# Attention with a memory, then a three-way max layer: weights assembled in PSUM, queries loaded twice, softmax sums by unit, another instruction order

## The chip, the cores and the metric

The kernel runs on one core of one Trainium2 chip. The core has a matrix engine (TensorE, PE in the profile; PEld is its loading of stationary operands), a vector engine (VectorE, DVE), a scalar engine (ScalarE, ACT), a general engine (GpSimd, POOL) and a queue for transfers (SyncE, SP). Each engine works through its own list of instructions in order, and engines wait for one another by semaphores. SBUF is the working memory with 128 partitions. PSUM holds eight banks of 512 float32 values per partition; matmuls write there. The metric is the device time of one execution in microseconds, less is better.

## The reference

Four batches, eight heads, 576 positions, 64 values per head. Causal attention is mixed with a read from a memory by a gate per head, and the result goes through a layer that takes the largest of three products:

```python
scores = q @ k^T / sqrt(D), causal          # B, H, S, D = 4, 8, 576, 64
a = exp(scores - max); a /= a.sum(-1) + 1e-9
local = a @ v
q_p = where(q > 0, q, exp(q) - 1) + 1       # phi(q)
mem_out = (q_p @ M_prev) / (q_p . z_prev + 1e-6)
g = sigmoid(beta)                            # one per head
x = (g * mem_out + (1 - g) * local)          # [2304, 512]
h = max(x @ w1, x @ w2, x @ w3)              # each [512, 768]
out = h @ w_out                              # [768, 512]
```

## The kernel before

**Tiling.** A batch is cut into two halves of the sequence: positions 0 to 319 (a "top" block of 64 rows and two units of 128) and 320 to 575 (two units of 128). A pair is one batch, one half and two heads, so there are 32 pairs and 64 steps of one head each. Pairs 0 to 7 are batch 0. The program (loop at line 890) goes through the steps. In step n it computes the scores of head n, transposes the probabilities of head n-1, multiplies by the values for the pair that ended in step n-2, and prepares the next pair. Once the four pairs of a half are done, the half's layer ("MoE" in the code) is queued: 18 upward products (6 column blocks times w1, w2, w3) of 12 matmuls each, and two or three downward products. They are handed out by a quota over the next eight steps (`run_moe`, line 873), so matmuls of the layer fill the time between those of attention.

**Split numbers.** For accuracy, most operands of matmuls are split into a high part (fp32r, a rounded float32) and a low part, the rest. A product is then three matmuls: high x high, low x high, high x low.

**Weights (`load_weights`, line 503).** The weights come in 24 chunks of 128 x 512 (18 of w1, w2, w3, 6 of w_out), read as 64-bit words in two 32-bit halves. For each chunk ScalarE scales the upper half into a tile `g` in SBUF. VectorE shifts `g` left by 3, ors in the lower half's upper bits (line 517), and ors in the sign (line 521). So a float32 is put together from the halves. Then ScalarE or VectorE makes the high part, and GpSimd or VectorE subtracts for the low part. One chunk each is prepared in steps 4 to 8 (`EARLY_STEPS`), and from then on two before each upward product (`PER_PIECE`), so the program lists all of them before the eleventh product. The raw chunks go through a ring of three buffers `r_w`, in which later also the raw keys and queries of pairs 8 to 31 lie.

**Queries and keys.** For pairs 0 to 3 the product of queries and keys is one float32 matmul. From pair 4 on a query tile `qs` holds 64 features twice over 128 partitions, since the keys' high and low parts lie in the two halves of the partitions. In pairs 4 to 7 the queries are transposed on PE, from pair 8 (`FLIP`) on VectorE in 32 x 32 blocks, after eight loads that place keys and queries. Both heads of a pair lie in the two halves of one transposed tile. So `split_in` (line 629) makes high and low part on the 64 partitions where a head lies, and then copies both across to the other 64 (line 642).

**Softmax.** `scores` masks and finds the maximum on VectorE, ScalarE takes the exponential with its sum. After the second unit of a head, VectorE adds 1e-9 to both units' sums and takes both reciprocals (`inverse`, line 678), and GpSimd multiplies both units by them and by the gate (`normal`, line 684). `phi` (line 529) works out phi(q) and its product with z: a reduction on VectorE, then an add of 1e-6 and a reciprocal.

**PSUM.** Eight banks: two for scores (`bs`), two for transposes (`bt`), one for the value product (`bv`), three for the layer (`bm`).

**Order of the instructions.** Nothing is issued as it is written. A planner (`Plan`) notes each operation with its operands, and `emit` (line 243) then goes through a simulated time: each operation has a cost (line 147) and delays after its inputs (`AFTER`, line 78), and each engine takes, among what is ready, what stands first in the program. Where an operation may run on one of two engines, the planner picks the one that would finish first, VectorE with a penalty of 1000 ns (`PEN`). Early on, where PE would idle over 400 ns, small "filler" matmuls are put in (line 280). They end when the bank that they write, the third of `bm`, is used for the first time. Nearly all operations are issued by line 297, so groups in the profile are told apart by the tiles: `g` and `rw` are weights, `wh`, `wl`, `woh`, `wol` their high and low parts, `p` probabilities, `pt` their transposes, `sum` softmax sums, `nn` phi's norms, `rk` transposed keys and queries, `k` the split keys, `t` the layer's maximum.

Of the kernel before, what the change touches and what calls it, by code (L numbers as in the profile page):

```python
# [67 lines left out]
class Plan:  # L68
# [18 lines left out]
    PEN = {"dve": 1000}  # L87

# [111 lines left out]

    def note(self, can):
# [41 lines left out]
    def emit(self):  # L243
# [6 lines left out]
        last = 0.0  # L250

        def place(op):
# [13 lines left out]
        for _ in self.ops:  # L266
# [56 lines left out]
def attention_memory_moe(ctx, tc, q, k, v, m_prev, z_prev, beta, w1, w2, w3, w_out, out):  # L323
# [14 lines left out]
    EARLY_STEPS, PER_PIECE = range(4, 9), 2  # L338
# [23 lines left out]
    r_e = Ring(cp, 2, [128, 384], F32, "phe")  # L362
    r_f = Ring(cp, 2, [128, 384], F32, "phf")

    r_k = Ring(cp, 2, [128, 512], F32, "rk")
    r_q0 = Ring(cp, 2, [128, 3, 2, D], F32, "rq")
# [11 lines left out]
    r_sum = Ring(cp, 6, [128, 2, 2], F32, "sum")  # L378
# [6 lines left out]
    b_m = Ring(ps, 3, [128, 512], F32, "bm")  # L385
# [13 lines left out]
    def load_qk(pi):  # L399
# [12 lines left out]
        else:  # L412
            t = f(r_w.next())
            r["k"], r["qt"] = t[:, : hf.n], t[:, 512 : 512 + hf.n]
            for src, to in ((k, r["k"]), (q, r["qt"])):
                for i in range(4):
# [3 lines left out]
                            b, 2 * hp + i // 2, hf.t0 : hf.t0 + hf.n, 32 * (i % 2) : 32 * (i % 2) + 32  # L420
                        ].rearrange("(c p) d -> p c d", p=32),
                    )
        t = r_q0.next()[:, : len(hf.blocks)]
        if hf.top:
            P.sp.dma_start(out=t[:, 0], in_=q[b, hs, 0:128, :].rearrange("h p d -> p h d"))
        for e in range(2):
            t0 = hf.t0 + hf.units[0][1]
            P.sp.dma_start(
                out=t[:, hf.top :, e],
                in_=q[b, 2 * hp + e, t0 : t0 + 256, :].rearrange("(c p) d -> p c d", p=128),  # L430
            )
        r["q"] = t
# [36 lines left out]
    nc.gpsimd.tensor_copy(out=qs_all[:, :64], in_=mask[:, :64])  # L469
    for e in range(2):  # L470
# [32 lines left out]
    def load_weights(n):  # L503
        for _ in range(min(n, len(wchunks))):
            src, dh, dl = wchunks.popleft()
# [6 lines left out]
            bits = g.bitcast(U32)  # L512
            P.act.activation(out=g, in_=f(words[:, :, 1]), func=AF.Copy, scale=2.0**-111)
# [8 lines left out]
                out=bits, in0=words[:, :, 1], scalar=0x80000000, in1=bits,  # L522
                op0=ALU.bitwise_and, op1=ALU.bitwise_or,
            )
            P.copy(("act", "dve"), out=dh, in_=gv)
            P.combine(("pool", "dve"), ALU.subtract, out=dl, in0=gv, in1=f(dh))


    def phi(pi):
# [7 lines left out]
        ev, fv = (  # L537
# [168 lines left out]
    def scores(pi, e, u):  # L706
# [21 lines left out]
        if i == 0:  # L728
            return
# [256 lines left out]
```

## Time and profile before

| | us |
|---|---|
| median of 3 runs | 558.21 (553.44 to 559.76) |
| the profiled execution | 556.39 |
| its span, first to last instruction | 554.6 |
| PE busy, PE weight loads busy | 517.9, 447.2 |
| VectorE, ScalarE, GpSimd busy | 318.7, 362.9, 340.5 |

The mean granted TensorE clock is 0.982 of full speed. Of the chain of work that ended last, the page gives PE 66%, VectorE 14%, ScalarE 7%, GpSimd 4%. Groups in the profile read: line, engine, operation, output <- inputs, sizes, count, then busy time in us, mean ns of one, idle time of the engine just before them and what ended it.

### The profile page before, as it was taken

To read this page: it belongs to the slowest core of one execution; us is meant where nothing else is said; L and a number is where in the kernel's file an instruction comes from. 1 tells how busy PE (TensorE), PEld (TensorE's weight loads), DVE (VectorE), ACT (ScalarE), POOL (GpSimd) and SP (SyncE) were. 2 spreads that over 40 slices of the span, in tenths; PEclk is the share of its full clock that TensorE was granted. 3 is DMA by queue.
4 is the path that set the end of the run, shared out by engine and by line. 5 is a ranking of instruction groups with operands and counts; after the bars stand their busy time and mean duration, and the time that the engine had idled before them with its cause. 6 is when DMAs were issued, how large, how long until landed. Compare 5 with 4: busy or idle time off the path is not lost.

```text
span 554.6 us, 10756 instructions
## 1 busy us (share of the span) xinstructions
PE 517.9 (93%) x3546; PEld 447.2 (81%) x3546; DVE 318.7 (57%) x984; ACT 362.9 (65%) x958; POOL 340.5 (61%) x488
## 2 busy tenths in 40 slices
PE   8989788787898999999999989999899999999997
PEld 6556666675587878998789978898799889998997
DVE  3597989998878646555445445645655354331110
ACT  5686778766698767766677757777777684543111
POOL 4587697797688665666866666766676465332120
PEclk9996899898999999999999999999999999999999
DMA  5464354543434542212441223221211110001001
GB/s 120 133 176 115 84 178 143 157 142 117 93 68 80 96 99 63 45 38 47 107 82 30 41 67 80 49 39 32 70 30 34 26 59 19 20 1 39 20 1 40
DMA packets 128728, 39.91 MB, mean 72 GB/s; under 512 B 115744, under 2 KB 125216, under 8 KB 128672
## 3 DMA queue, kind: packets, MB, share of 16 engines
q1 hardware_dynamic: 128672, 39.22, 29.7%
q8 instruction: 28, 0.46, 0.4%
q14 instruction: 28, 0.23, 0.1%
HBM read 34.48 MB, written 4.72 MB: 71 GB/s over the span
## 4 chain that ended last, share of the span: by engine, by line
PE 66%; DVE 14%; ACT 7%; POOL 4%; issue 4%; DMA 3%; SPq 1%; DVEq 0%; POOLq 0%; ACTq 0%
PE bm L297 41%; PE bt L297 9%; PE bs L297 8%; PE bv L297 7%; DVE g L297 4%; POOL p L297 2%; DVE p L297 2%; ACT p L297 2%; DVE nn L297 2%; SPq L297 1%; DVE k L297 1%; ACT k L297 1%; ACT pt L297 1%; DMA rv<-in_v_dram 1%; DVE qs L297 1%
## 5 line engine op out<-in xcount | busy, mean ns | idle before, releaser
L297 PE MATMUL bm<-xh,wh 128*128 128x320 f32 (+1 forms) x576 | 178.6, 311 | 1.2 <-DVE wh L297 0.7
L297 PE MATMUL bm<-xh,wl 128*128 128x320 f32 (+1 forms) x576 | 173.5, 301 | 0.0
L297 PE MATMUL bm<-xl,wh 128*128 128x320 f32 (+1 forms) x576 | 173.1, 301 | 0.0
L297 POOL TENSOR_SCALAR p<-p,sum,gb 128x192 f32<-128x192 f32 (+3 forms) x128 | 96.2, 761 | 37.8 <-DVE sum L297 33.6
L297 PEld LDWEIGHTS bm<-xh,wh 128*128 128x128 f32 x576 | 110.4, 192 | 5.5 <-issue 3.0
L297 PEld LDWEIGHTS bm<-xl,wh 128*128 128x128 f32 x576 | 110.5, 192 | 1.5 <-issue 1.0
L297 PEld LDWEIGHTS bm<-xh,wl 128*128 128x128 f32 x576 | 110.3, 192 | 1.0 <-issue 0.8
L297 DVE TENSOR_TENSOR t<-bm,t 128x320 f32<-128x320 f32 (+1 forms) x96 | 43.5, 453 | 116.3 <-PE bm L297 108.4
L297 ACT ACTIVATE p<-p,st 128x576 f32<-128x576 f32 (+4 forms) x144 | 84.4, 587 | 21.4 <-DVE st L297 20.3
L297 PE MATMUL bt<-ident,p 128*128 128x128 f32 x464 | 77.1, 284 | 18.5 <-ACT pt L297 5.9
L297 PE MATMUL bs<-k,qs 128*128 128x448 f32 (+3 forms) x336 | 71.9, 315 | 10.5 <-DVE st L297 10.0
L297 PEld LDWEIGHTS bt<-ident,p 128*128 128x128 f32 x464 | 56.4, 144 | 30.3 <-POOL p L297 10.6
L297 DVE CUSTOM_DVE_ANT_0 p<-bs,mask 128x192 f32<-128x192 f32 (+3 forms) x128 | 60.6, 475 | 31.6 <-PE bs L297 30.8
L297 ACT COPY pt<-bt 128x512 f32<-128x512 f32 (+3 forms) x171 | 68.8, 418 | 13.0 <-PE bt L297 10.4
L297 PEld LDWEIGHTS bs<-k,qs 128*128 128x128 f32 x336 | 50.6, 188 | 15.1 <-DVE st L297 13.0
L297 POOL TENSOR_TENSOR qs<-rk,qs 64x256 fp32r<-64x256 f32 (+1 forms) x40 | 32.2, 805 | 40.0 <-ACT qs L297 21.2
L297 POOL TENSOR_TENSOR p<-phf,nn 128x128 f32<-128x128 f32 (+1 forms) x96 | 37.7, 398 | 25.6 <-PE bt L297 18.8
L297 POOL TENSOR_TENSOR hl<-t,hh 128x256 fp32r<-128x256 f32 x36 | 27.4, 761 | 33.2 <-ACT hh L297 33.2
L297 POOL TENSOR_TENSOR xl<-kt,xh 128x256 fp32r<-128x256 f32 (+1 forms) x28 | 24.1, 862 | 36.3 <-ACT kt L297 36.0
L297 DVE SCALAR_TENSOR_TENSOR g<-rw,g 128x512 uint32<-128x512 uint32 x48 | 43.3, 911 | 0.2
L297 ACT CAST qs<-rk 64x256 fp32r<-64x256 f32 (+1 forms) x47 | 20.2, 430 | 34.5 <-PE bs L297 33.2
L297 PE MATMUL bv<-pt,rv 128*64 128x256 f32 (+1 forms) x384 | 42.3, 352 | 0.0
(101 smaller groups left out, 893.9 us busy)
## 6 DMA issues: line engine op xcount, KB each, us to landing
rw<-in_moe_w_dram SPq DMA_DIRECT2D x18, 512.0 KB, 3.8
rq<-in_q_dram SPq DMA_DIRECT2D x80, 64.0 KB, 2.3
rv<-in_v_dram SPq DMA_DIRECT2D x32, 128.0 KB, 2.7
out_dram<-g SPq DMA_DIRECT2D x15, 256.0 KB, 2.1
rw<-in_moe_w_out_dram SPq DMA_DIRECT2D x6, 512.0 KB, 3.3
rv<-in_v_dram SPq DMA_DIRECT2D x32, 64.0 KB, 2.2
rw<-in_k_dram SPq DMA_DIRECT2D x48, 40.0 KB, 2.1
rw<-in_q_dram SPq DMA_DIRECT2D x48, 40.0 KB, 2.0
```

The source lines that it names most:

```text
L297: getattr(getattr(self.nc, self.ENGINES[e]), op.fn)(**op.args)
```

## The change

**Weights.** The scaled word, the shift and the first or now lie in a PSUM bank; only the last or writes `g` in SBUF. The bank comes from the layer's three: any of them for the first eight chunks (`SPREAD`), then the second and third in turn. The layer's ring `b_m` has only the first bank until all chunks are listed; then the other two are added. The high part is always made by ScalarE, the low part always by GpSimd. One chunk is listed in each of the steps 3 to 8, then one (not two) before each upward product, so the last stands before the eighteenth.

**Queries.** From pair 8 on, each head's queries are loaded twice, into both halves of the partitions, and each head has a transpose of its own on VectorE: twelve loads and three transposes for a pair where there were eight and two. In pairs 4 to 7 the untransposed queries are loaded twice side by side, and PE transposes each head's doubled block. `split_q` makes high and low part on all 128 partitions; the copy across is gone. The transposed tiles have a ring of three.

**Sums.** Each unit has its own sum: add, reciprocal and multiplication follow each unit's exponential. In `phi` the product with z has a 65th column that holds 1e-6, set once, so the reduction adds it and the separate add is gone; that tile has one buffer now.

**Order.** In the planner's time a PE operation is ready 500 ns later after another engine's (`SLACK`), and VectorE operations with two SBUF inputs, or plain copies and one-input operations wholly in SBUF, do not overlap with GpSimd (`shares`). The fillers write the bank of `bv`, so they end at the first value product. Splitting the keys of pairs 0 to 3 stays where it was in the program.

```diff
+    SLACK = 500
+    def shares(eng, name, kw):
+        if eng == "pool":
+            return True
+        if eng != "dve":
+            return False
+        aps = [a for a in kw.values() if isinstance(a, bass.AP) and a.shape[-1] > 1]
+        inputs = [a for k, a in kw.items() if k in ("in_", "in0", "in1") and a.space != PSUM]
+        if len(inputs) > 1:
+            return True
+        return name in ("tensor_scalar", "tensor_copy") and not any(a.space == PSUM for a in aps)
...
-                ready = max([0.0] + [o.end + self.AFTER[o.eng][e] for o in op.deps])
+                ready = max([0.0] + [
+                    o.end + self.AFTER[o.eng][e] + self.SLACK * (e == "pe" and o.eng != "pe")
+                    for o in op.deps
+                ])
...
+            if self.shares(e, op.fn, op.args):
+                op.at = max(op.at, port[other[e]])
+                port[e] = op.at + op.cost
...
-    EARLY_STEPS, PER_PIECE = range(4, 9), 2
+    EARLY_STEPS, PER_PIECE = range(3, 9), 1
+    SPREAD = 8
...
-    b_m = Ring(ps, 3, [128, 512], F32, "bm")
+    bm = Ring(ps, 3, [128, 512], F32, "bm").tiles
+    b_m = Ring.of(bm[:1])
...
-            for src, to in ((k, r["k"]), (q, r["qt"])):
+            loads = [(k, r["k"], (0, 1))]
+            for e in range(2):
+                r["qt", e] = t[:, 320 + 320 * e :][:, : hf.n]
+                loads.append((q, r["qt", e], (e, e)))
+            for src, to, hd in loads:
...
+            bank = bm[i % 3 if i < SPREAD else 1 + i % 2]
-            bits = g.bitcast(U32)
-            P.act.activation(out=g, in_=f(words[:, :, 1]), func=AF.Copy, scale=2.0**-111)
+            bits = bank.bitcast(U32)
+            P.act.activation(out=bank, in_=f(words[:, :, 1]), func=AF.Copy, scale=2.0**-111)
...
-                out=bits, in0=words[:, :, 1], scalar=0x80000000, in1=bits,
+                out=g.bitcast(U32), in0=words[:, :, 1], scalar=0x80000000, in1=bits,
...
-            P.copy(("act", "dve"), out=dh, in_=gv)
-            P.combine(("pool", "dve"), ALU.subtract, out=dl, in0=gv, in1=f(dh))
+            P.act.copy(out=dh, in_=gv)
+            P.pool.tensor_tensor(out=dl, in0=gv, in1=f(dh), op=ALU.subtract)
+        if not wchunks and len(b_m.tiles) == 1:
+            b_m.tiles += bm[1:]
+            b_m.at = 1
...
-        P.dve.tensor_reduce(out=nv, in_=ev, axis=AX.X, op=ALU.add)
-        P.dve.tensor_scalar(out=nv, in0=nv, scalar1=1e-6, scalar2=None, op0=ALU.add)
+        P.dve.tensor_reduce(out=nv, in_=zv, axis=AX.X, op=ALU.add)
...
+    def split_q(pi, e, src):
+        r = raw[pi]
+        n = HALVES[pairs[pi][1]].n
+        r["qs", e] = r_q.next()
+        qs = qs_all[:, r["qs", e] : r["qs", e] + 640].rearrange("p (a x) -> p a x", a=2)
+        P.copy(("act", "dve"), out=qs[:, 0, :n], in_=src)
+        P.combine(
+            ("dve", "pool") if pi >= FLIP else ("dve",), ALU.subtract,
+            out=qs[:, 1, :n], in0=src, in1=f(qs[:, 0, :n]),
+        )
...
-                P.copy(("dve", "act"), out=qs[hi_, :, :n], in_=qs[lo, :, :n])
...
-        exponential(p, st[:, len(cuts) - 1 : len(cuts)], sums[:, 0, i : i + 1])
-        if i == 0:
-            return
-        inverse(sums)
-        for i, u in enumerate(hf.units):
-            p = r["pbuf", e][:, i * hf.pitch + D : i * hf.pitch + D + u[3]]
-            normal(p, sums[:, 1, i : i + 1], gb[:, 1, 2 * hp + e : 2 * hp + e + 1])
+        exponential(p, st[:, len(cuts) - 1 : len(cuts)], total)
+        normal(p, total, gb[:, 1, 2 * hp + e : 2 * hp + e + 1])
...
-        out=b_m.tiles[2][:32, :64], lhsT=mask[:, :32], rhs=mask[:, :64], start=True, stop=True
+        out=b_v.tiles[0][:32, :64], lhsT=mask[:, :32], rhs=mask[:, :64], start=True, stop=True
```

More of the change, by code (lines that the diff above doesn't have):

```diff
@@ L250, in emit @@
         last = 0.0
+        port = {"pool": 0.0, "dve": 0.0}
+        other = {"pool": "dve", "dve": "pool"}
         def place(op):
@@ L377, in attention_memory_moe @@
     r_st = Ring.of(stats[:, 2 * i : 2 * i + 2] for i in range(8))
-    r_sum = Ring(cp, 6, [128, 2, 2], F32, "sum")
+    sums = tile_([128, 12], F32, "sum")
+    r_sum = Ring.of(sums[:, i : i + 1] for i in range(12))
     r_nn = Ring(cp, 2, [128, 2, 4, 2], F32, "nn")
@@ L427, in load_qk @@
             t0 = hf.t0 + hf.units[0][1]
[L428 to L432, printed above, removed]
+            for i in range(twice):
+                P.sp.dma_start(
+                    out=t[:, hf.top :, e, D * i : D * i + D],
+                    in_=q[b, 2 * hp + e, t0 : t0 + 256, :].rearrange("(c p) d -> p c d", p=128),
+                )
+        r["q"] = t[:, :, :, :D]
     per_batch = {}
@@ L504, in load_weights @@
         for _ in range(min(n, len(wchunks))):
+            i = 4 * NF - len(wchunks)
             src, dh, dl = wchunks.popleft()
@@ L596, in transpose_in @@
         n = hf.n
-        if pi >= FLIP:
-            src = r_k.next()[:, :n]
-            P.dve.transpose(out=src, in_=r["k" if nm == "k" else "qt"])
+        if pi >= FLIP and nm == "k":
+            src = r_kq.next()[:, :n]
+            P.dve.transpose(out=src, in_=r["k"])
+        elif pi >= FLIP:
+            for e in range(2):
+                src = r_kq.next()[:, :n]
+                P.dve.transpose(out=src, in_=r["qt", e])
+                split_q(pi, e, src)
+            return
         elif nm == "k":
@@ L610, in transpose_in @@
         else:
-            t = b_t.next()
-            for i, (q0, rows) in enumerate(hf.blocks):
-                P.pe.transpose(
-                    out=t[:, q0 : q0 + rows],
-                    in_=r["q"][:rows, i].rearrange("p h d -> p (h d)"),
-                    identity=ident[:rows, :rows],
-                )
-            src = t[:, :n]
+            for e in range(1 if pi < SPLIT else 2):
+                t = b_t.next()
+                for i, (q0, rows) in enumerate(hf.blocks):
+                    x = r["qq"][:rows, i]
+                    P.pe.transpose(
+                        out=t[:, q0 : q0 + rows],
+                        in_=x.rearrange("p h d -> p (h d)") if pi < SPLIT else x[:, e],
+                        identity=ident[:rows, :rows],
+                    )
+                src = t[:, :n]
+                if pi >= SPLIT:
+                    split_q(pi, e, src)
+            if pi >= SPLIT:
+                return
         if pi < SPLIT:
@@ L676, in exponential, with normal @@
         P.act.activation(out=p, in_=p, func=AF.Exp, scale=-1.0, bias=least, accum_out=total)
[L678 to L687 removed]
+    def normal(p, total, gate):
+        P.dve.tensor_scalar(out=total, in0=total, scalar1=1e-9, scalar2=None, op0=ALU.add)
+        P.dve.reciprocal(out=total, in_=total)
+        P.pool.tensor_scalar(out=p, in0=p, scalar1=total, scalar2=gate, op0=ALU.mult, op1=ALU.mult)
     def scores_top(pi):
@@ L713, in scores @@
         st = r_st.next()
-        if i == 0:
-            r["sum"] = r_sum.next()
-        sums = r["sum"]
+        total = r_sum.next()
         cuts = [(0, ext)] if ext <= 512 else [(0, ext // 2), (ext // 2, ext)]
```

72 lines of the change are left out of this document (30 added, 42 removed).

## The prediction, made before the changed kernel ran

> **What bounds the kernel now.** I read the page's busy shares and slices first, then busy time by stage, then the groups of the stage that stood out. On the page (engines, then tenths of each of 40 slices, then the granted TensorE clock):
>
> ```profile
> span 554.6 us, 10756 instructions
> PE 517.9 (93%) x3546; PEld 447.2 (81%) x3546; DVE 318.7 (57%) x984; ACT 362.9 (65%) x958; POOL 340.5 (61%) x488
> PE   8989788787898999999999989999899999999997
> DVE  3597989998878646555445445645655354331110
> PEclk9996899898999999999999999999999999999999
> ```
>
> PE looks like the bound everywhere, but a busy PE is modelled from pipelined matmuls. VectorE is at 9 tenths in slices 4 to 10 only. So I cut the span into stages: first steps, weight preparation, the change-over to the second batch, the long middle, the MoE tail.
>
> ```profile
> core 0: us, PE busy (x) PEld busy (x) DVE busy (x) ACT busy (x) POOL busy (x), PEclk, DMA share, GB/s
> 0.00:28.00 28.00, 26.17 (x137) 17.39 (x137) 13.26 (x59) 16.38 (x46) 13.65 (x32) 1.00 0.53 125
> 28.00:146.00 118.00, 98.94 (x580) 76.24 (x580) 107.83 (x256) 86.42 (x213) 94.17 (x101) 0.91 0.49 135
> 146.00:200.00 54.00, 48.40 (x366) 43.02 (x365) 39.28 (x135) 42.96 (x122) 38.78 (x61) 1.00 0.44 84
> 200.00:515.00 315.00, 307.89 (x2191) 275.40 (x2190) 153.27 (x524) 210.55 (x564) 189.44 (x290) 1.00 0.22 48
> 515.00:555.00 40.00, 36.48 (x280) 35.19 (x278) 5.10 (x12) 6.64 (x16) 4.45 (x6) 1.00 0.07 21
> ```
>
> From 200 us on PE is the bound: weight loads are busy 275.4 of 315 us, 0.87, and no other engine passes 0.67. From 28 to 146 us they reach 0.65, and VectorE is busy 107.8 of 118 us, 0.91. There VectorE sets the pace, GpSimd at 0.80 behind it. The groups of that stage, VectorE first, then GpSimd (count, busy us, mean ns, idle before):
>
> ```profile
> L297 DVE SCALAR_TENSOR_TENSOR g<-rw,g 128x512 uint32<-128x512 uint32 x48 | 43.3, 911 | 0.2
> L297 DVE TENSOR_SCALAR g<-g 128x512 uint32<-128x512 uint32 x24 | 16.6, 691 | 0.9 <-ACT g L297 0.9
> L297 DVE TENSOR_TENSOR wol<-g,woh 128x512 fp32r<-128x512 f32 x3 | 3.8, 1280 | 3.2 <-ACT woh L297 3.2
> L297 DVE CAST wh<-g 128x512 fp32r<-128x512 f32 x4 | 2.0, 492 | 0.1
> L297 DVE TENSOR_SCALAR sum<-sum 128x2 f32<-128x2 f32 x12 | 3.6, 299 | 0.1
> L297 DVE RECIPROCAL sum<-sum 128x2 f32<-128x2 f32 x12 | 1.8, 151 | 0.0
> L297 DVE TENSOR_SCALAR nn<-nn 128x6 f32<-128x6 f32 x3 | 1.2, 416 | 0.0
> L297 DVE TENSOR_SCALAR nn<-nn 128x4 f32<-128x4 f32 x4 | 1.0, 254 | 0.0
> ...
> L297 POOL TENSOR_TENSOR wl<-g,wh 128x512 fp32r<-128x512 f32 x17 | 24.4, 1440 | 4.3 <-ACT wh L297 2.9 <-DVE wh L297 1.3
> L297 POOL TENSOR_SCALAR p<-p,sum,gb 128x576 f32<-128x576 f32 x8 | 12.1, 1510 | 0.0
> L297 POOL TENSOR_SCALAR p<-p,sum,gb 128x448 f32<-128x448 f32 x8 | 9.2, 1151 | 5.9 <-DVE sum L297 5.9
> ```
>
> All 24 weight chunks fall in this stage, and their VectorE passes are 43.3 + 16.6 + 3.8 + 2.0, some 66 of its 107.8 us. The same GpSimd operations in the long middle, and one place of the timeline inside the stage (start, duration):
>
> ```profile
> L297 POOL TENSOR_SCALAR p<-p,sum,gb 128x576 f32<-128x576 f32 x24 | 21.1, 881 | 0.0
> L297 POOL TENSOR_SCALAR p<-p,sum,gb 128x448 f32<-128x448 f32 x24 | 17.3, 720 | 14.6 <-DVE sum L297 14.2
> ```
>
> ```profile
> 65.25 3.53 POOL L297 TENSOR_SCALAR p<-p,sum,gb 128x448 f32<-128x448 f32 x2 [1.66 <-DVE sum L297]
> 65.31 2.85 DVE L297 SCALAR_TENSOR_TENSOR g<-rw,g 128x512 uint32<-128x512 uint32 x4
> ```
>
> The normalisation that takes 881 ns later takes 1510 ns here. At 65 us two of them last 3.53 us, exactly over four weight passes. So the two engines hold each other up in this stage, beyond their own work.
>
> The Trainium skill, page "SBUF — State Buffer", section "Who interferes with whom", names the cause: a VectorE operation with two SBUF inputs takes a port that GpSimd needs, and one with a PSUM input does not. The trace agrees as to the first half (1510 against 881 ns); no row here shows the second.
>
> **Weights in PSUM (24 chunks).** The shifted word lies in a PSUM bank, so both two-input passes have one PSUM input. The nearest rows are VectorE's maximum against a PSUM bank, and its plain copy out of PSUM:
>
> ```profile
> L297 DVE TENSOR_TENSOR t<-bm,t 128x320 f32<-128x320 f32 x48 | 23.3, 485 | 48.0 <-PE bm L297 47.9
> L297 DVE TENSOR_TENSOR t<-bm,t 128x256 f32<-128x256 f32 x48 | 20.2, 420 | 68.3 <-PE bm L297 60.4 <-ACT phf L297 3.2 <-ACT pt L297 2.8
> L297 DVE COPY pt<-bt 128x384 f32<-128x384 f32 x7 | 3.9, 552 | 0.4 <-PE bt L297 0.4
> ```
>
> 65 ns for 64 more elements gives 1.02 ns each, so 512 elements take 420 + 256 x 1.02 = 680 ns. 48 passes at 680 instead of 911 save 11.1 us. The shift, now in and out of PSUM, is priced from the copy: 552 + 128 x 1.02 = 682 ns, against 691: nothing. The bounds for the shift come from its own spread (min/median/max ns), with the weight subtraction's for below:
>
> ```profile
> L297 DVE TENSOR_SCALAR g<-g x24: 401/532/1499, 30.0 to 140.9; 128x512 uint32<-128x512 uint32 x24
> L297 POOL TENSOR_TENSOR wl<-g,wh x17: 1272/1294/1792, 34.7 to 121.0; 128x512 fp32r<-128x512 f32 x17
> ```
>
> Undisturbed it takes 401 ns in SBUF, so PSUM could be dearer by 24 x 0.28 = 6.7 us; if GpSimd is what stretches it to 691, it is free. The rows bear out the second (one reached 1499), so I keep zero and leave 6.7 us to the range.
>
> The Trainium skill, page "VectorE: DVE Perf Modes", section "Why PSUM operands drop a tier", speaks against the change: a PSUM operand bars a one-input float32 pass from its double rate. The minimum of 401 ns for 512 elements fits a double rate in SBUF. By the page's table (120 cycles and one per element at 0.96 GHz) the shift would take an estimated 658 ns, 24 x 0.26 = 6.2 us more than undisturbed; the sum below would then be 543 instead of 537.
>
> Casts and subtractions of weights leave VectorE: 3.8 + 2.0 = 5.8 us less. GpSimd gets four more subtractions at 1294 ns, 5.2 us.
>
> **Softmax sums unit by unit; the added column in phi.** Two-column adds and reciprocals become twice as many of one column. The 12 + 12 of this stage cost 5.4 us now. A reciprocal I leave at 151 ns, an add between that and its 299: I take 151, since the 299 holds waits for GpSimd, so 24 x 0.30 = 7.2 us, +1.8 (bound +5.4). The added 1e-6 column drops an add, 1.2 + 1.0 = 2.2 us. With the single buffer that phi keeps, ScalarE waits for the previous reduction, one pair earlier: nothing.
>
> **Sum for 28 to 146 us.** VectorE: 107.8 - 11.1 - 5.8 + 1.8 - 2.2 = 90.5, and one or two transposes more (below) make it 91. GpSimd: 94.2; the normalisations fall to 881 and 720 ns, 8 x 0.63 + 8 x 0.43 = 8.5 less; 17 weight subtractions at their median, 2.5 less; 5.2 more: 88. ScalarE stays near 86. VectorE at its present share, 91 / 0.91 = 100, would shorten the stage by 18 us. But three engines now stand within 5 us of each other and feed each other, so I take a share of 0.875: 104 us, 14 less. At 0.80 it is 4 less. PE would allow it: at its pace of the middle, 76.2 / 0.87 = 88 us.
>
> **Queries loaded twice.** The copies across partitions go: over the run
>
> ```profile
> L297 ACT CAST qs<-qs 64x512 fp32r<-64x512 f32 x28 | 17.3, 618 | 2.5 <-DVE qs L297 1.8
> L297 ACT CAST qs<-qs 64x640 fp32r<-64x640 f32 x23 | 16.7, 726 | 0.9 <-POOL qs L297 0.4
> L297 DVE STREAM_TRANSPOSE rk<-rw 128x320 f32<-128x320 f32 x24 | 12.0, 505 | 1.7 <-POOL qs L297 0.7 <-POOL k L297 0.6
> 157.44 1.88 SPq L297 DMA_DIRECT2D rw<-in_k_dram x4
> ```
>
> 34.0 us of ScalarE, and a link of 0.6 to 0.7 us before each head's scores. It costs VectorE a transpose for each of 24 pairs (24 x 0.505 = 12 us at most) and SP four more loads a pair, 1.88 us, ahead of the v loads, weights and outputs queued behind. Pairs 8 to 31 take 315 / 24 = 13 us or more each, and a load is made one pair ahead, so this is hidden; if SP is late, 1.9 us are due at the change-over. There, 146 to 200 us, PE waits for the attention chain: weight loads at 0.80, 43.0 / 0.87 = 49.4 could do, so at most 4.6 us are to be had. I take 3 less (from 5 less to 3 more). Pairs 4 to 7 get their second copy of the queries by two more loads and two more PE transposes each, while VectorE is the bound: nothing. In the middle ScalarE and VectorE are off the path: PE has 315 - 307.9 = 7 us of idle time to give.
>
> **Order.** The planner puts PE work 500 ns later after other engines, so that matmuls with ready operands stand ahead. In the middle that can only take from those 7 us: 2 less (7 less to 4 more, if half a microsecond shows at some of the unit hand-overs). The tail is pure MoE: unchanged. In the first 28 us one chunk comes a step earlier and unit sums save a wait: zero. Fillers now stop at the first value product, so these go:
>
> ```profile
> L280 PE MATMUL bm<-mask x8: 219/219/243, 31.4 to 38.8; 128*32 128x64 f32 x8
> ```
>
> The clock fell to 0.6 in slice 4 even with them; PE has room there: zero, up to 2 more.
>
> **One accumulator bank.** Until the chunks are loaded, each of the 18 first MoE products waits on PE for VectorE or ScalarE to empty bank 0, and attention products stand behind it. Emptying now, and one product's length:
>
> ```profile
> L297 DVE TENSOR_TENSOR t<-bm,t x12: 461/480/491, 68.5 to 130.9; 128x320 f32<-128x320 f32 x12
> L297 ACT COPY t<-bm x6: 404/430/439, 65.1 to 121.3; 128x320 f32<-128x320 f32 x6
> 233.80 1.76 PE bm L297 x12
> 105.84 1.12 PE L297 MATMUL bs<-k,qs 128*128 128x448 f32 x2 [3.15 <-DVE st L297]
> ```
>
> 18 emptyings from 65.1 to 130.9 us are 3.9 us apart. One bank needs 1.76 + 0.48 = 2.2 us and the hand-overs; VectorE's queue may hold it 1.6 us more before it is slower than now. I cost it at nothing, covered by that slack.
>
> **Total.** 0 - 14 - 3 - 2 - 0 = -19: a span of 535.6. The profiled execution took 556.39 us around its 554.6, so 1.8 is added: 537. That execution is 0.3% under the median of 558.21, which is within the runs' spread.
>
> **Rivals.** *No relief:* the long weight passes come from something that PSUM does not cure, say from the two engines' hand-overs; then 911 stays and the shift gets dearer by up to 6.7. VectorE saves only 5.8 + 2.2 - 1.8, and nothing if the shift pays in full; change-over and middle give 3. About 554. For it: the pass's 911 ns is not the sum of one GpSimd operation; against: the timeline at 65 us. Chance 0.17. *The single bank decides:* from a turn of 3.9 us on, 17 turns add 1.7 us for each 0.1. With VectorE as late as in the row above (3.15 us), a turn is 5.4 us, 25 us more; at half that excess, 4.7, the stage is 14 us longer than now in spite of the cheaper weights: 554.6 + 14 - 4 + 1.8 = 566. For it: VectorE's 0.91 and 3.15 us; against: its load falls to 0.875 and the planner knows the bank. Chance 0.12. *Everything helps:* the stage at its present share (-18), all of the change-over and the middle (-5, -7): 526 or less. Chance 0.10.
>
> **Numbers.** The forecast of 537, from 527 to 549 (stage from 18 to 4 less, the shift's 6.7 inside), has 0.61. For 8 in 10 the range goes from 522 to 556, which takes in "no relief". One per cent of 558 is 5.6 us, about what a measurement of this kernel can tell from no change: faster is under 552.6, slower over 563.8. Faster: 0.61 + 0.10, and 0.04 of "no relief". Same: 0.13 of it. Slower: 0.12.
>
> **What would show it.** In the new profile the weight passes should read near 680 ns, the 576-wide normalisation of the first stage near 900, and the last chunk should end some 14 us earlier. Copies across partitions are gone, and SP shows twelve loads for pairs 8 on. If VectorE is under 0.8 and PE waits there for bank 0, the single bank decides; if the passes stay at 900, no relief. Weight loads above 0.90 in the middle would mean that the order is worth more than I gave it.

## The result and the profile after

The changed kernel takes 533.3 us (median of 4 runs, 532.5 to 535.0); the kernel before took 557.3 beside it (553.4 to 559.8). The ratio is 0.958, with a 95% interval of 0.952 to 0.964. The forecast was 537, in a range of 522 to 556. The profiled execution took 532.99 us around a span of 531.2, so 23.4 us of span went.

The page of the kernel after, the same lines that were shown of the kernel before:

```profile
span 531.2 us, 11153 instructions
PE 509.4 (96%) x3602; PEld 445.1 (84%) x3602; DVE 283.8 (53%) x1048; ACT 336.1 (63%) x942; POOL 332.5 (63%) x505
PE   9879999989989899999999999999999999999997
DVE  3667999987675354465455354445754454240110
PEclk9966999999999899999999999999999999999999
```

VectorE has lost 34.9 us of work, and its stretch at eight and nine tenths ends with the ninth slice, not the thirteenth. PE is at 96% of a shorter span. The first slices of PE's clock are worse than before, not better.

Busy time by stage, the columns as in the prediction:

```profile
28.00:146.00 118.00, 108.19 (x678) 85.11 (x677) 97.81 (x308) 93.98 (x251) 89.93 (x124) 0.92 0.58 147
146.00:200.00 54.00, 49.15 (x349) 43.71 (x348) 28.51 (x119) 35.65 (x110) 38.02 (x59) 0.97 0.49 95
200.00:515.00 315.00, 315.00 (x2294) 286.69 (x2294) 141.68 (x558) 185.74 (x525) 185.71 (x286) 1.00 0.24 51
```

These windows stand at fixed times, so more of the work now falls into the early ones, and VectorE's 97.8 us cannot be set against the 91 of the sum. What can be read is PE: it does 677 weight loads between 28 and 146 us where it did 580, hardly more than before in the change-over (43.7 us of them, 43.0 before), and in the middle it is never idle (7.1 us before), with weight loads busy 286.7 of 315 us, 0.91. Against the same windows before, that is 8.9 us more of weight loads from 28 to 146 us, 0.7 more from 146 to 200 and 11.3 more from 200 to 515.

To see where the time went I followed one event per pair: the start of the copy of its value product out of `bv`. From ScalarE's timeline, the events of pairs 4, 7, 9, 11 and 31, of the kernel before:

```profile
74.20 0.37 ACT L297 CAST xh<-bv 128x256 fp32r<-128x256 f32 x1
...
142.77 0.37 ACT L297 CAST xh<-bv 128x256 fp32r<-128x256 f32 x1 [1.93 <-PE bv L297]
...
177.43 0.41 ACT L297 CAST xh<-bv 128x320 fp32r<-128x320 f32 x1
...
205.54 0.43 ACT L297 CAST xh<-bv 128x320 fp32r<-128x320 f32 x1 [0.78 <-PE bv L297]
...
512.88 0.37 ACT L297 CAST xh<-bv 128x256 fp32r<-128x256 f32 x1 [1.51 <-PE bv L297]
```

and of the kernel after:

```profile
73.78 0.37 ACT L320 CAST xh<-bv 128x256 fp32r<-128x256 f32 x1 [0.27 <-PE bv L320]
...
132.17 0.38 ACT L320 CAST xh<-bv 128x256 fp32r<-128x256 f32 x1 [0.18 <-PE bv L320]
...
158.92 0.43 ACT L320 CAST xh<-bv 128x320 fp32r<-128x320 f32 x1 [0.18 <-PE bv L320]
...
192.25 0.43 ACT L320 CAST xh<-bv 128x320 fp32r<-128x320 f32 x1
...
489.17 0.37 ACT L320 CAST xh<-bv 128x256 fp32r<-128x256 f32 x1 [1.51 <-PE bv L320]
```

The lead over the kernel before is 0.4 us at pair 4, 10.6 at pair 7, 18.5 at pair 9, 13.3 at pair 11 and 23.7 at pair 31. The stages of the sum end at 146 and 200 us; in the kernel before, pair 7 (142.77 us) and pair 11 (205.54 us) stand nearest to these. By these marks the first steps gain nothing, the weight stage gains 10, the change-over 3 and the middle 10. Between them the lead rises to 18.5 at pair 9, and 5 of that are lost again by pair 11.

A pair's lead is not all time of PE. Up to pair 9, PE's weight loads were busy for 116.5 us in the kernel before and 112.8 in the kernel after (91.4 and 90.1 up to pair 7, 140.7 and 138.9 up to pair 11). So part of the 18.5 is work that PE still has to do in the kernel after. The sum was right by 4 us; its parts were not all right, above all the middle.

The groups of the weight stage, 28 to 146 us, VectorE's and then GpSimd's:

```profile
L320 DVE SCALAR_TENSOR_TENSOR bm<-rw,bm 128x512 uint32<-128x512 uint32 x23 | 15.7, 688 | 0.0
L320 DVE SCALAR_TENSOR_TENSOR g<-rw,bm 128x512 uint32<-128x512 uint32 x23 | 15.5, 679 | 0.1
L320 DVE TENSOR_SCALAR bm<-bm 128x512 uint32<-128x512 uint32 x22 | 15.1, 690 | 2.7 <-ACT bm L320 2.7
...
L320 DVE RECIPROCAL sum<-sum 128x1 f32<-128x1 f32 x35 | 5.1, 151 | 0.0
...
L320 DVE TENSOR_SCALAR sum<-sum 128x1 f32<-128x1 f32 x34 | 4.9, 144 | 4.0 <-ACT p L320 3.5
...
L320 POOL TENSOR_TENSOR wl<-g,wh 128x512 fp32r<-128x512 f32 x17 | 21.8, 1288 | 8.1 <-ACT wh L320 8.0
...
L320 POOL TENSOR_SCALAR p<-p,sum,gb 128x576 f32<-128x576 f32 x8 | 6.6, 826 | 6.6 <-DVE sum L320 2.5 <-ACT qs L320 1.8 <-ACT bm L320 1.3
```

The prices of the weight stage held: the passes at 679 to 688 ns (680 forecast, 911 before), the shift at 690 (682 forecast), the wide normalisation at 826 (881 forecast, 1510 before), the one-column add at 144 (151 taken). The last shift of a chunk starts at 120.9 us, where it started at 140.9:

```profile
L320 DVE TENSOR_SCALAR bm<-bm x24: 675/691/700, 21.2 to 120.9; 128x512 uint32<-128x512 uint32 x24
...
L320 DVE SCALAR_TENSOR_TENSOR bm<-rw,bm x24: 675/689/697, 22.0 to 121.7; 128x512 uint32<-128x512 uint32 x24
...
L320 DVE SCALAR_TENSOR_TENSOR g<-rw,bm x24: 670/678/689, 22.8 to 122.4; 128x512 uint32<-128x512 uint32 x24
```

### The profile page after: what moved, and what is told of

It reads as the page before. It is cut to its first block, busy times and chain, and to the rows that moved or that the text cites. A ratio compares the mean times of both kernels' runs of the same rounds, so it can differ in the third digit from the quotient of the medians.

```text
span 531.2 us, 11153 instructions
## 1 busy us (share of the span) xinstructions
PE 509.4 (96%) x3602; PEld 445.1 (84%) x3602; DVE 283.8 (53%) x1048; ACT 336.1 (63%) x942; POOL 332.5 (63%) x505
## 4 chain that ended last, share of the span: by engine, by line
PE 75%; ACT 6%; DMA 6%; DVE 4%; SPq 4%; issue 2%; POOL 2%; DVEq 0%; POOLq 0%; ACTq 0%
PE bm L320 49%; PE bv L320 9%; PE bt L320 8%; PE bs L320 8%; SPq L320 4%; DMA rw<-in_moe_w_dram 2%; DMA rw<-in_k_dram 1%; DMA rw<-in_q_dram 1%; ACT p L320 1%; PE bv L300 1%; ACT pt L320 1%; DVE g L320 1%; DVE bm L320 1%; ACT wh L320 1%; ACT k L320 1%
## 5 line engine op out<-in xcount | busy, mean ns | idle before, releaser
L320 POOL TENSOR_SCALAR p<-p,sum,gb 128x192 f32<-128x192 f32 (+3 forms) x128 | 87.5, 685 | 46.7 <-DVE sum L320 34.5
L320 ACT ACTIVATE p<-p,st 128x192 f32<-128x192 f32 (+4 forms) x144 | 84.7, 588 | 17.6 <-DVE st L320 16.6
L320 PE MATMUL bt<-ident,p 128*128 128x128 f32 x464 | 73.6, 279 | 11.5 <-ACT pt L320 7.9
L320 ACT COPY pt<-bt 128x384 f32<-128x384 f32 (+3 forms) x189 | 74.5, 417 | 10.9 <-PE bt L320 10.2
L320 PE MATMUL bs<-k,qs 128*128 128x448 f32 (+2 forms) x336 | 69.9, 310 | 1.3 <-DVE st L320 1.1
L320 POOL TENSOR_TENSOR qs<-rk,qs 128x256 fp32r<-128x256 f32 (+1 forms) x42 | 34.2, 816 | 33.6 <-ACT qs L320 18.7
L320 POOL TENSOR_TENSOR hl<-t,hh 128x256 fp32r<-128x256 f32 x42 | 31.0, 739 | 34.1 <-ACT hh L320 34.1
L320 DVE STREAM_TRANSPOSE rk<-rw 128x320 f32<-128x320 f32 (+1 forms) x72 | 34.2, 476 | 30.0 <-POOL qs L320 10.6
L320 ACT CAST qs<-rk 128x256 fp32r<-128x256 f32 (+1 forms) x47 | 20.1, 431 | 36.1 <-PE bs L320 35.3
L320 PEld LDWEIGHTS bv<-pt,rv 128*64 128x64 f32 x384 | 27.9, 141 | 16.9 <-issue 2.9
```

The lines of the kernel that those rows point to most:

```text
L320: getattr(getattr(self.nc, self.ENGINES[e]), op.fn)(**op.args)
```

## The experiments

The theory was that of the sum: cheaper weight passes shorten the weight stage, the rest is small. Its rivals were that another part of the change carries the gain (the new listing of the chunks, the order, the sums), and that something in it costs. Each edit below is made on the kernel after unless it says otherwise. The lead at a pair is always that of the copy out of `bv` over the kernel before.

### The weights back in SBUF (e1, e9)

```diff
-            bits = bank.bitcast(U32)
-            P.act.activation(out=bank, in_=f(words[:, :, 1]), func=AF.Copy, scale=2.0**-111)
+            bits = g.bitcast(U32)
+            P.act.activation(out=g, in_=f(words[:, :, 1]), func=AF.Copy, scale=2.0**-111)
```

> The changed kernel (533.3 us), with one thing undone: the word is scaled, shifted and put together in the SBUF tile g as before, while the single accumulator bank, the listing of one chunk per product and all else stay. Contention theory (the weight passes with two SBUF inputs and GpSimd hold each other up): the two-input passes go from 680 ns back to some 850 to 950, the 576-wide normalisation before 146 us from 826 ns to over 1200, and the time rises by 10 to 18 us, to 543 to 551. Rival (the gain is from the new order and the spread listing): passes may get longer, but the time stays within 4 us of 533.

545.6 us (544.9 to 548.4), 0.983 of the kernel before [0.977, 0.988]; the kernel after stands at 0.958. Tile `g` (duration min/median/max, first and last start):

```profile
L320 DVE SCALAR_TENSOR_TENSOR g<-rw,g x48: 652/821/1666, 21.0 to 145.8; 128x512 uint32<-128x512 uint32 x48
...
L320 DVE TENSOR_SCALAR g<-g x24: 402/556/1101, 20.3 to 143.6; 128x512 uint32<-128x512 uint32 x24
```

and GpSimd's groups of the stage:

```profile
L320 POOL TENSOR_SCALAR p<-p,sum,gb 128x448 f32<-128x448 f32 x8 | 10.0, 1248 | 1.7 <-ACT g L320 0.8 <-DVE sum L320 0.7
L320 POOL TENSOR_SCALAR p<-p,sum,gb 128x576 f32<-128x576 f32 x8 | 8.3, 1040 | 1.4 <-DVE nn L320 1.4
```

Two lines bring the disturbance back: passes from 652 to 1666 ns where PSUM has 670 to 697, the wide normalisation at 1040 instead of 826 ns (over 1200 was expected), the last chunk 23 us later. The lead at pair 9 falls from 18.5 to 3.0. *No relief* falls.

The shift in SBUF is stretched as well. In the kernel before, the nine shifts that start while GpSimd is idle take 0.40 to 0.42 us, and the thirteen that take 0.5 us or more (up to 1.50) all start while a GpSimd operation runs.

The Trainium skill, page "SBUF — State Buffer", section "Who interferes with whom", says that VectorE and GpSimd share one pair of SBUF ports as an exclusive lock. Now the trace shows the half that it could not show before the change: with one input in PSUM, no stretching of either engine is seen (826 ns beside passes that vary by 27 ns).

The same with all three accumulator banks given back to the layer from the start, since the weights don't need them:

```diff
-    b_m = Ring.of(bm[:1])
+    b_m = Ring.of(bm)
```

> The kernel with weights in the SBUF tile (545.6 us), but the products get all three accumulator banks from the start, which SBUF leaves free. This prices the single bank by itself. My prediction held it to cost nothing: 544 to 547. Rival (products wait on bank 0 and hold up the attention behind them): 535 to 541. The gap to the changed kernel's 533.3 that is left is the worth of PSUM by itself.

546.4 us (545.3 to 552.6), 0.988 [0.980, 0.996], against 545.6 with one bank. Two more banks bring nothing, with the weights in SBUF. With the weights in PSUM the one bank was judged by waits alone: in the kernel after, PE's waits for a bank that VectorE has yet to empty are small between 28 and 146 us (us, times, longest), for matmuls and for weight loads:

```profile
PE bm L320 <- DVE t L320: 3.0, 4, 1.0
...
PEld bm L320 <- DVE t L320: 4.5, 5, 1.2
PEld bs L320 <- DVE st L320: 1.7, 4, 0.7
```

The longest is 1.2 us, under the 1.6 of slack that the prediction counted. *The single bank decides* falls.

### PSUM alone, and the old listing (e6, e5)

On the kernel before, the weights' PSUM edits alone, with one accumulator bank until all chunks are listed and the fillers on the bank of `bv`:

```diff
+            bank = bm[i % 3 if i < SPREAD else 1 + i % 2]
...
-            bits = g.bitcast(U32)
-            P.act.activation(out=g, in_=f(words[:, :, 1]), func=AF.Copy, scale=2.0**-111)
+            bits = bank.bitcast(U32)
+            P.act.activation(out=bank, in_=f(words[:, :, 1]), func=AF.Copy, scale=2.0**-111)
...
-                out=bits, in0=words[:, :, 1], scalar=0x80000000, in1=bits,
+                out=g.bitcast(U32), in0=words[:, :, 1], scalar=0x80000000, in1=bits,
...
+        if not wchunks and len(b_m.tiles) == 1:
+            b_m.tiles += bm[1:]
```

> The kernel before with weights in PSUM alone: scaled word, shift and first or in the bank, the ring of one accumulator bank until all chunks are listed, fillers on the bank of the value product; old listing, old queries, sums and order, copies and subtractions on either engine. Theory (PSUM frees VectorE and GpSimd by itself): 540 to 546 against 556.5. Rival (PSUM pays only with the listing and the order, since one bank with two chunks per product holds the products up): 552 or more.

552.7 us (10 runs, 548.7 to 555.9), 0.998 [0.993, 1.003]: no change. Yet the passes are as cheap as in the kernel after, VectorE's work over the whole run falls from 318.7 to 302.9 us, and the last pass starts at 125.4 instead of 143.6 us. Tile `g`, then the stage's window, then pair 9 on ScalarE's timeline:

```profile
L297 DVE SCALAR_TENSOR_TENSOR g<-rw,bm x24: 671/682/689, 33.3 to 125.4; 128x512 uint32<-128x512 uint32 x24
```

```profile
28.00:146.00 118.00, 99.12 (x545) 73.53 (x541) 100.93 (x268) 95.72 (x238) 83.32 (x111) 0.86 0.56 145
```

```profile
175.53 0.43 ACT L297 CAST xh<-bv 128x320 fp32r<-128x320 f32 x1 [0.27 <-PE bv L297]
```

Pair 9 is only 1.9 us earlier, and pair 7, at 148.72 us, is 5.9 later. PE does fewer weight loads in the stage than before (541 against 580). The weights are done 18 us earlier, and the attention does not profit. This is where the sum's theory fell: it let VectorE's load set the length of the stage.

A second cause is possible in e6. PE waits there between 28 and 146 us for the one bank, which it does not do in the kernel before:

```profile
PEld bm L297 <- DVE t L297: 6.1, 4, 2.2
```

PSUM with the old listing and three banks was not run, so how much of e6 is the bank's stays open.

The counterpart keeps everything of the change but the listing of the chunks:

```diff
-    EARLY_STEPS, PER_PIECE = range(3, 9), 1
+    EARLY_STEPS, PER_PIECE = range(4, 9), 2
```

> The changed kernel with the old listing of the chunks: one in each of the steps 4 to 8, then two before each product, so all are listed before the eleventh. PSUM, bank ring, queries, sums and order as changed. Theory (spreading the chunks over 18 products lets attention and products share VectorE, and with the weight passes in PSUM gives most of the gain that undoing PSUM alone, 12 us, does not explain): 540 to 550. Rival (the listing is worth nothing, VectorE's work is the same in all): 530 to 536.

542.9 us (540.4 to 544.5), 0.977 [0.974, 0.981]: two numbers cost 9.6 us. Tile `g`, then the wait of PE's weight loads between 28 and 146 us for the scores' maxima, then pair 9 on the timeline:

```profile
L320 DVE SCALAR_TENSOR_TENSOR g<-rw,bm x24: 675/680/690, 24.0 to 114.6; 128x512 uint32<-128x512 uint32 x24
```

```profile
PEld bs L320 <- DVE st L320: 10.4, 7, 4.0
```

```profile
172.12 0.43 ACT L320 CAST xh<-bv 128x320 fp32r<-128x320 f32 x1
```

The weights end 8 us *earlier* than in the kernel after, and pair 9 comes 13 us later. With two chunks listed ahead of each product, the chunks stand ahead of the attention in the program, and so on VectorE. PE then waits 10.4 us for scores that VectorE has yet to reduce (1.7 us in the kernel after, 7.5 in the kernel before), up to 4.0 at a time. Its waits for the one bank are no longer than in the kernel after (3.9 us against 4.5), so here the bank is not the cause.

The four cases together, the lead at pair 9 in us:

| | two chunks a product | one chunk a product |
|---|---|---|
| weights in SBUF | 0 (before) | 3.0 (e1) |
| weights in PSUM | 1.9 (e6), 5.3 (e5) | 18.5 (after) |

(e6 has none of the change's other parts; e1 and e5 have all of them. The profiled execution of e5 lies 2.5 us under its median and that of e6 2.3 over it, which leaves the picture as it is. The other parts with neither edit were not run.) At pair 7 the picture is the same: -9.0 (e1), -5.9 (e6), -2.1 (e5) and 10.6 (after). Each is a single execution, but 18.5 stands far from the others. Neither edit is worth much there without the other. PSUM shortens the chunks; the listing lets the attention into the room that they leave.

### The order (e2, e8)

```diff
-    SLACK = 500
+    SLACK = 0
...
-            if self.shares(e, op.fn, op.args):
+            if False:
```

> The changed kernel with the planner's two new rules off: no 500 ns for PE after other engines, and no exclusion of VectorE and GpSimd in the planner's time. The operations are the same, their order is the old planner's. My prediction gave the order 2 us: 535. Rival (the order is what gained the middle and the change-over, where the changed kernel won some 10 us): 541 or more, with weight loads in the middle back to 0.87 to 0.88 from 0.91.

533.4 us (528.0 to 536.4; 532.3 without the longest run), 0.956 [0.949, 0.963]: the same time as with the order. From pair 12 to pair 31 the lead grows by 4.7 us, where the kernel after gains 7.5; at pair 9 it is 23.0, 4.5 more than in the kernel after. But this profiled execution is the shortest of its runs, so some of its lead may be that. The kernel after also waits for its queries (next section), which may hide what the order is worth. So the same edit was made again on the kernel with the old queries and old sums (b1, below):

> Queries and sums as before (the kernel of 527.1 us), and also the planner's two rules off, so what is left of the change is PSUM with one accumulator bank, the listing, the fixed engines for casts and subtractions, phi's added column and the fillers. The kernel of 527.1 gained 7.3 us on the kernel before between the thirteenth and the last pair. Theory (this gain of the middle comes from the order): it falls to 0 to 2 us, and the time is 529 to 535, the start a little faster than with the rules, as with the other kernel without them. Rival (phi's dropped add and single buffer do it): the middle still gains 5 us or more and the time is 522 to 527.

534.0 us (530.7 to 537.5), 0.962 [0.954, 0.969], against 527.1 (526.4 to 528.5) with the order. The middle, 200 to 515 us, without the order (e8):

```profile
200.00:515.00 315.00, 312.21 (x2249) 281.06 (x2248) 138.59 (x483) 202.46 (x545) 178.75 (x277) 1.00 0.20 44
```

and with it (b1):

```profile
200.00:515.00 315.00, 315.00 (x2291) 287.40 (x2291) 143.08 (x480) 203.10 (x545) 178.44 (x274) 1.00 0.20 43
```

With the order PE has no idle time in the middle (2.8 us without) and does 43 more weight loads in it (2248 to 2291). From pair 12 to 31 the lead grows by 7.3 us with the order and by 1.7 without. So some 5.6 us of the order's worth lie there, in an execution of e8 that is 3 us longer than its median. Why the order gains 6.9 us of the median with the old queries and nothing with the doubled ones stays open: the fronts of e2 and e8 differ by as much as their executions do from one another.

### The queries and the sums (e4, e3, b1)

The queries as they were: eight loads and two transposes a pair, and the copy across partitions (the core of the edit):

```diff
-            loads = [(k, r["k"], (0, 1))]
-            for e in range(2):
-                r["qt", e] = t[:, 320 + 320 * e :][:, : hf.n]
-                loads.append((q, r["qt", e], (e, e)))
-            for src, to, hd in loads:
+            r["k"], r["qt"] = t[:, : hf.n], t[:, 512 : 512 + hf.n]
+            for src, to in ((k, r["k"]), (q, r["qt"])):
...
+                P.copy(("dve", "act"), out=qs[hi_, :, :n], in_=qs[lo, :, :n])
```

> The changed kernel with the queries as before: eight loads and two transposes a pair, the halves copied across partitions by ScalarE or VectorE (56 copies, some 38 us). My prediction gave this part most of 3 us at the change-over (146 to 200 us) and nothing in the middle: 535 to 537. Rival (hidden, since PE is the bound from 200 us on): within 1 us of 533. Other rival (the links of 0.7 us before each head's scores were on the path in the middle as well): 540 or more.

526.6 us (525.8 to 528.4), 0.947 [0.943, 0.951]: 6.7 us *faster* than the kernel after, which none of the three expectations had. The part of the change that was to spare 34 us of ScalarE costs time. In the kernel after, VectorE's transposes wait for their loads between 125 and 200 us (us, times, longest):

```profile
DVE rk L320 <- DMA rw<-in_k_dram: 8.2, 4, 3.2
DVE rk L320 <- DMA rw<-in_q_dram: 7.1, 5, 2.7
```

and SP, which issues them, is hardly ever free from 120 to 172 us (its waits add up to 4.2 us, none over 0.4). Two of its rows (start, duration):

```profile
152.11 3.85 SPq L320 DMA_DIRECT2D rw<-in_q_dram  x8
...
168.45 3.85 SPq L320 DMA_DIRECT2D rw<-in_q_dram  x8
```

A load takes SP 0.48 us, so a pair's twelve take 5.8 us, and value loads, outputs and the other copies of queries come on top. Counted over SP's timeline from 120 to 172 us, it issues 26 loads of keys here, those of 6.5 pairs, and 41 with the old queries, those of 10 pairs. The chain of waits from 146 to 200 us, by line, after and with the old queries (e4):

```profile
by line: PE bm L320 25.0%; SPq L320 16.3%; DMA rw<-in_k_dram 14.5%; issue 6.1%; PE bt L320 5.2%; PE bs L320 4.8%; ACT k L320 4.4%; DMA rq<-in_q_dram 4.1%; ACT phe L320 3.0%; ACT p L320 3.0%; DVE rk L320 2.6%; PE bv L320 2.5%; ACT pt L320 2.
```

```profile
by line: PE bm L320 67.0%; PE bs L320 11.5%; PE bv L320 11.3%; PE bt L320 10.3%
```

With the old queries that stretch is PE's alone, and the lead holds: 18.8 us at pair 9, 18.9 at pair 11. From pair 7 to pair 11 it gains 8.8 us, where the kernel after gains 2.7. The copies across partitions, 34 us of ScalarE, hide behind PE.

The sums as they were, added and inverted for both units at once:

```diff
-        exponential(p, st[:, len(cuts) - 1 : len(cuts)], total)
-        normal(p, total, gb[:, 1, 2 * hp + e : 2 * hp + e + 1])
+        exponential(p, st[:, len(cuts) - 1 : len(cuts)], sums[:, 0, i : i + 1])
+        if i == 0:
+            return
+        inverse(sums)
```

> The changed kernel with softmax sums per head again: add, reciprocal and both units' multiplications after the second unit. My prediction: the unit sums cost VectorE 2 to 5 us before 146 us and save a wait of one unit for GpSimd, so 533 within 3 us either way. Rival (the earlier multiplication of the first unit is what shortened the chain in the middle): 3 to 8 us longer, and PE waits for GpSimd's p more than now.

529.9 us (528.1 to 532.5), 0.953 [0.948, 0.958]: 3.4 us under the kernel after, with intervals that overlap, and a little outside the 3 us expected. Whether that belongs to the sums shows with the queries out of the way, so b1 takes both back:

> The changed kernel with both parts undone that cost time: queries as before and softmax sums per head. If the two effects add (6.7 us and 3.4 us): 523. If both are the same slack in VectorE: 526 to 527.

527.1 us (526.4 to 528.5), 0.948 [0.946, 0.951], against 526.6 with the old queries alone. So the sums unit by unit do nothing by themselves. What they cost in the kernel after, if anything, depends on the late loads.

### Only the loads (e7)

Is it the third transpose or the loads? On e4, four more loads a pair from pair 8 on, which nothing reads (192 positions each instead of 256 or 320):

```diff
+            for i in range(4):
+                P.sp.dma_start(
+                    out=t[32 * i : 32 * i + 32, 320:512].rearrange("p (c d) -> p c d", d=32),
+                    in_=q[
+                        b, 2 * hp + i // 2, hf.t0 : hf.t0 + 192, 32 * (i % 2) : 32 * (i % 2) + 32
+                    ].rearrange("(c p) d -> p c d", p=32),
+                )
```

> The changed kernel with the queries as before (526.6 us), and four more loads a pair from pair 8 on that nothing reads: the same number of load instructions as the changed kernel has, 0.6 to 0.75 of their bytes, no third transpose. Theory (SP's issue of some 17 loads a pair at 0.48 us each runs behind between 120 and 200 us, and that is what the doubled queries lose): 530 to 534, with SP busy without a break from 120 to 190 us. Rival (the loss comes from the third transpose on VectorE or from its ring of three): 526 to 528.

533.6 us (532.0 to 534.4), 0.959 [0.956, 0.962]: the whole loss is back with no transpose added. VectorE's waits, 125 to 200 us:

```profile
DVE rk L320 <- DMA rw<-in_k_dram: 11.6, 4, 3.8
```

The lead goes from 15.0 us at pair 9 to 12.5 at pair 11; the kernel after has 18.5 and 13.3. It is the loads. Whether it is their issue on SP or their transfer, e7 does not tell apart; that the DMA engines are busy only 0.49 of 146 to 200 us in the kernel after speaks for the issue.

### Fillers and transfers in the plan (e10, e11)

The first 74 us gained nothing (0.4 us at pair 4), and PE's clock there had fallen. Granted clock from 24 to 56 us, third number from the right, before, after, and with the old queries (e4):

```profile
24.00:56.00 32.00, 30.12 (x153) 18.99 (x153) 26.92 (x87) 24.04 (x72) 24.90 (x38) 0.84 0.51 134
```

```profile
24.00:56.00 32.00, 25.47 (x103) 14.27 (x103) 23.44 (x89) 24.83 (x75) 23.81 (x38) 0.68 0.59 149
```

```profile
24.00:56.00 32.00, 25.09 (x97) 14.49 (x97) 23.73 (x86) 25.99 (x77) 22.84 (x37) 0.59 0.49 131
```

On e4, the fillers write bank 0 of the layer and so may go on for longer, and they fill gaps from 200 ns on:

```diff
-FILL_GAP, FILL_FROM = 400, 450
+FILL_GAP, FILL_FROM = 200, 450
...
-    SPREAD = 8
+    SPREAD = 0
...
-        out=b_v.tiles[0][:32, :64], lhsT=mask[:, :32], rhs=mask[:, :64], start=True, stop=True
+        out=bm[0][:32, :64], lhsT=mask[:, :32], rhs=mask[:, :64], start=True, stop=True
```

> The changed kernel with the queries as before (526.6 us); chunks use only the second and third accumulator bank from the start, so the first is free for products, the fillers write that first bank and so go on until the first product, and they are put in from gaps of 200 ns on. TensorE's granted clock is at 0.5 to 0.6 for most of 28 to 55 us in the changed kernel. Theory (this clock holds up the first pairs): the clock stays above 0.8 there, pair 4 is done 3 to 6 us earlier, 521 to 524. Rival (attention's chain and the transfers set the first 60 us, whatever the clock): within 1.5 us of 526.6.

```profile
24.00:56.00 32.00, 26.67 (x133) 16.07 (x134) 26.13 (x98) 28.92 (x83) 25.18 (x39) 0.80 0.56 151
```

The clock rises from 0.59 to 0.80, and the time stays: 526.7 us (525.0 to 536.1; 526.0 without the longest run), 0.948 [0.942, 0.953], against 526.6. The profiled execution is ahead (2.4 us at pair 4, where e4 is 1.3 behind the kernel before), the median is not. So a gain from the clock isn't shown. The edit also moves the chunks off the first bank, so it does not test the clock alone.

In the first 60 us ScalarE also waits some 4 us for raw weights (3.9 us in the kernel after from 12 to 60 us). On e10 the planner's price of a transfer was raised, so that work on them stands later:

```diff
-        return size / 360 * (2 if piece < 512 else 1)
+        return size / 230 * (2 if piece < 512 else 1)
```

> The kernel with the first accumulator bank free for products and more fillers (profiled 525.0 us), with one more thing: the planner holds a transfer to move 230 bytes per ns, not 360, so ScalarE's scaling passes stand later in its list. Weight chunks land a median of 4.6 us after issue in the changed kernel, and ScalarE waited 6.7 us for them, in order, with attention's copies behind. Theory (these waits hold up the first pairs): ScalarE waits for chunks under 1 us in all, pair 4 is done 1 to 3 us earlier, 521 to 524. Rival (attention's own chain sets the first 60 us; a later order only moves the wait): 525 to 528.

526.4 us (6 runs, 525.5 to 532.7), 0.947 [0.943, 0.952]: ScalarE's waits for raw weights are gone (0.9 us were left in e10), and the time is the same. The expected 1 to 3 us at pair 4 did not come (76.18 us, where e10 has 71.79). What sets the first 60 us stays open.

The kernels with the old queries (e4, b1, e10, e11) take 526.4 to 527.1 us and can't be told apart. All beat both kernels; e4, the simplest edit, is 1.3% under the kernel after.

## Why the prediction was right, and where its steps were not

The time, 533.3, is 4 us below the 537 forecast, and inside the 527 to 549 of the likeliest case. It came about in another way.

- **The weight stage, 14 less: 10 at pair 7, 18 at pair 9, and for half of the reason.** The prices were right (680 ns forecast and 679 to 688 measured; shift at no net cost; normalisations near their later 881). The step that failed is "VectorE at its present share ... would shorten the stage". PSUM alone takes 15.8 us off VectorE's work in the run and 18 us off the last chunk, and leaves the time at 0.998 (e6). The listing, one chunk a product, stood in the change and not in the sum at all. Without it the kernel after loses 9.6 us of its time, without PSUM 12.3 (e5, e1). So it was luck that a share of 0.875 gave about the right figure.
- **The shift in PSUM, zero kept of a possible 6.7: right.** The 690 ns measured stand against 691 before. With the word in SBUF again a shift takes 402 ns at the least and 556 in the median (e1). The Trainium skill, page "VectorE: DVE Perf Modes", section "Why PSUM operands drop a tier", is borne out as far as 402 against 690 ns goes. The 543 us that followed from it did not come, since beside GpSimd the shift had lost its rate already: 691 ns in the mean, and 0.40 to 0.42 us where it starts with GpSimd idle.
- **The change-over, 3 less: 3 less from pair 7 to pair 11, but in spite of the queries and not through them** (from pair 9 on the lead falls from 18.5 to 13.3). With the old queries the same stretch gives 8.8 (e4), so the right figure is luck. The step that failed is "a load is made one pair ahead, so this is hidden; if SP is late, 1.9 us are due". I set a pair's time of 13 us against the 1.88 us of four loads. The queue had to be counted whole: every load of a pair, and the backlog of the weight chunks' own loads and ring, which the raw keys and queries share (that last cause is argued, not tested). SP is hardly free for 50 us there. The doubled queries cost 6.7 us (e4), and four loads alone cost as much (e7).
- **The middle, 2 less: 10 less**, of which 2.9 come between pairs 11 and 12 (2.7 without the order too, in e8) and 7.5 after. The step that failed is "that can only take from those 7 us: 2 less". Between the marks of pairs 11 and 31 the profiles show 2151 matmuls in both kernels: 300.2 us busy and 7.1 idle before, 296.9 busy and none idle after. So all of the idle time went, where I took 2 of it, and PE's busy time fell by 3.3 us as well, which the sum did not foresee and whose cause stays open. Weight loads at 0.91 were the sign named for this, and with the old queries some 5.6 us there are the order's (e8). In the changed kernel as it is, the middle gains 2.8 us less without the order, but the whole time stays the same (e2).
- **Sums, casts, one bank, first steps, tail at nothing: right as totals.** The one bank costs nothing that is seen (e9, with the weights in SBUF), the sums nothing (b1), the first steps gain 0.4 us. The casts on ScalarE and phi's added column were not undone by themselves. With the fillers ended earlier the clock from 24 to 56 us is 0.68, where it was 0.84; up to 2 us were kept for that, and no cost is shown (e10).
- **Two readings were loose.** VectorE stands at 9 tenths in slices 3, 5, 7, 8 and 9, not in all from 4 to 10. And at 65 us the two normalisations take 3.53 us beside four passes that take 2.85, which is an overlap but not "exactly". The sum does not rest on either.
- **The rivals.** *No relief* fell by the passes, *the single bank decides* by PE's waits and e9. *Everything helps*, 526 or less, is about what the change gives once its queries are taken back: 526.6.

## What to carry to other kernels

Before crediting a cheaper operation with time, ask what is queued behind it, and whether the program's order lets the waiting work into the room that it leaves: here the cheaper passes were worth nothing (e6, with one bank for the layer) until the chunks were also spread out. Count a queue of transfers by everything that it issues in the worst stretch and not by the added loads against an average period; copies that hide behind a busy engine can be cheaper than loads that spare them. When a sum comes out right, undo its parts one by one: here 0, 14, 3 and 2 were really 0, 10, 3 and 10, and the 3 hid a loss of 6.7. Choose the marks of a stage where the sum ends it: at pair 9 instead of pair 7 the weight stage would have read 18.

## What the runs showed of the hardware that was not expected

- How evenly a VectorE pass runs with one input in PSUM: 670 to 697 ns over 48 passes, with GpSimd at work beside it; 652 to 1666 ns with both in SBUF.
- How dear a small load is to the queue that issues it: 0.48 us each on SP (eight in 3.85 us). Four more a pair made 7.0 us of the whole (533.6 in e7 against 526.6 in e4).
- How little a low clock of PE showed in the time here: granted 0.59 (e4) or 0.80 (e10) from 24 to 56 us, the medians differ by 0.1 us. e10 has other edits too, so the clock alone was not tested.
- That a one-input shift in SBUF takes 0.40 to 0.42 us when it starts with GpSimd idle, and up to 1.50 us when it starts behind a GpSimd operation.
